# Induced attention and a leaky feed-forward block on one core: a weight quarter loaded later, and a re-planned stage for the first two tiles

## The chip, the cores and the metric

The kernel runs on 1 core of one Trainium2 chip. The metric is the device time of one execution in microseconds (us). PE is the matrix engine (TensorE), ACT the scalar engine (ScalarE), DVE the vector engine (VectorE), POOL the GpSimd engine, and SP the sync engine, whose queue issues nearly all DMAs here.

## The reference

```
B, N, m, C = 4, 12480, 32, 128;  d_ff = 2048;  scale = 1 / sqrt(C)

def mab(q, kv):
    s = scale * (q @ kv^T);  s = s - s.max(-1)
    a = exp(s);  a /= a.sum(-1) + 1e-9
    return a @ kv
h   = mab(inducing, x)             # 32 induced rows of each batch
y   = mab(x, h)                    # attention of all 49920 rows over h
g   = y @ w_in;  g = max(0.01 * g, g)
out = g @ w_out
```

The inputs x and inducing are float32; w_in and w_out come as doubles and are turned into float32 on the chip.

## The kernel before

**What is computed where.** The attention of a row over its batch's 32 induced rows, h, is a softmax weight a of 32 numbers, so `y @ w_in` is `a @ (h @ w_in)`. The kernel makes `hw = h @ w_in` once for each batch, and a product with the first matrix then takes 32 rows of PE's array. Four such products with different hidden blocks f (128 of the 2048 units each) run beside each other on the four row groups of the array; line L1261 (`quarter`) issues these and most of the second products, which are cut into four row groups as well. Operands are kept as a high part and a rest (`ghi`/`glo`, `w_hi`/`w_lo`, `hwhi`/`hwlo`), so a product takes three passes. The slope of 0.01 is a linear term, `w12 = 0.01 * w_in @ w_out`, applied through h (`linear_part`, L1315 in the first stage).

**A tile** is 512 tokens; there are 98 (`NT`), two of them pairs of the batches' remainders. For each tile and f, ACT makes `ghi` from PSUM with a ReLU (L1227). Then either DVE makes `glo` (L1231, the near way), or ACT writes g to SBUF and POOL makes both `ghi` (a cast, L1514) and `glo` (L1516), the far way. `relu` chooses between them by the planner's clocks.

**The order in time.** (1) `first_batch` runs the attention of batch 0 over its rows by a hand-written order: PE transposes row tiles (L748), ACT and DVE copy them to `xT` (L754), PE makes the scores (L410), DVE their maxima (L423, L436, L455), ACT the exponentials, PE the values (L590). Its DMAs are all issued by SP at the start, one after the other: 25 row tiles, and behind those numbered in `LOADS` a quarter of w_in, or the first quarter of w_out. The numbers in `ROUNDS` set where the conversion of the weights from doubles (`from_double`) is put between: for each quarter ACT's `cv_a` (L213), DVE's `cv_b` (L219), `cv_a` (L224), `cv_b` (L231) and `cv_t` (L236), and POOL's sum (L242, into `w_in_sb` or `wraw`). (2) The stage of the first two tiles, `staged`: their first products in rounds of four f, and second products as whole-array matmuls (L1304), with the rest of w_out's conversion, its split (`w_hi` on ACT, L309, `w_lo` on POOL, L313), `w12` (L356) and a softmax of the second tiles (L949 to L999) between. (3) The loop over tiles 2 to 97. Here a planner, run while the program is built, gives every engine its instructions in the order of its own clocks. Work that needs PE's array in another shape (scores L410, values L590, spreads L497) waits until it is gathered into a break of the row-tiled stream; `WAITS` says for each break how long it is put off. (4) A tail for the last tile.

**The planner** does not measure: `spent(engine, ns)` advances a clock by a number written in the code, and these numbers set the order. In `best`, an engine takes what is ready first by them. DVE, ACT and POOL then run their instructions strictly in that order, so a wait of one instruction holds up all behind it.

```
LOADS = [4, 8, 12, 16, 20]
if i in LOADS:
    c = LOADS.index(i)
    raws.append(load_w_in(c) if c < NF // 4 else load_w_out(0))
...
useful = far < max(clock[DVE], start + RELU) + backlog(DVE) + LOW + BEHIND   # in the stage
useful = far <= wanted()                                                     # in the loop
```

Of the kernel before, what the change touches and what calls it, by code (L numbers as in the profile page):

```python
# [19 lines left out]
def induced_attention_then_leaky_ffn(  # L20
# [34 lines left out]
    while N - base >= 4 * TOK:  # L55
# [12 lines left out]
    HEAVY = 2  # L68
    PE, ACT, DVE, POOL, SP = "PE", "ACT", "DVE", "POOL", "SP"

    LOADS = [4, 8, 12, 16, 20]

# [21 lines left out]
    LANDED = 3800.0  # L94
    RELU, LOW, COPIED, ADDED, BLOCKS = 599.0, 691.0, 587.0, 691.0, 702.0
    FAR_HIGH, FAR_LOW, FAR_SUM = 613.0, 1297.0, 1299.0
    SETTLED = 75.0
    EARLY, PREFER, YIELDING, PATIENCE = 250.0, 0.0, 200.0, 6000.0
    IDLE, HURRY, APART, TAIL, WAITING, SOON = 1300.0, 1000.0, 60000.0, 5000.0, 3500.0, 3000.0
# [1 line left out]
    LINEAR = NF - 3  # L101
    SPREAD = 80.0
    WAITS = [
# [3 lines left out]
    ]  # L107
    AHEAD = 100.0
    CLOCKS = {ACT: 1500.0, DVE: 1150.0, POOL: 1800.0}
# [32 lines left out]
    clock = {ACT: 0.0, DVE: 0.0, POOL: 0.0, SP: 0.0}  # L142
# [4 lines left out]
    def spent(engine, ns, *after):  # L147
        if not timing[0]:
            return 0.0
        signal = TO_POOL if engine == POOL else SIGNAL  # L150
        end = max([clock[engine], now[0], *(a + signal for a in after)]) + ns
        clock[engine] = end - OVERLAP[engine]
        return end
# [45 lines left out]
    def from_double(raw, dst):  # L199

        n = dst.shape[1]
        low, high = raw[:, :, 0], raw[:, :, 1]
        a = sb.tile([P, n], I32, tag="aT", name="cv_a", bufs=4)
        b = sb.tile([P, n], I32, tag="aT", name="cv_b", bufs=4)  # L210
        tail = sb.tile([P, n], F32, tag="osb", name="cv_t", bufs=2)
        yield from new(ACT, 0.0)
        nc.scalar.mul(a.bitcast(F32), high.bitcast(F32), 2.0**-112)  # L213
        at = spent(ACT, 700.0)
        if not timing[0]:
            yield
        yield from new(DVE, 0.0)
        spent(DVE, 700.0)
        nc.vector.tensor_scalar(  # L219
            out=b, in0=high, scalar1=-0x80000000, scalar2=None, op0=ALU.bitwise_and  # L220
        )
        yield from old()
        yield from new(DVE, at)
        nc.vector.scalar_tensor_tensor(  # L224
            out=a, in0=a, scalar=3, in1=b, op0=ALU.logical_shift_left, op1=ALU.bitwise_or
        )
        at = spent(DVE, 800.0, at)
        yield from old()
        yield from new(DVE, at)
        spent(DVE, 600.0)  # L230
        nc.vector.tensor_scalar(  # L231
            out=b, in0=a, scalar1=-0x800000, scalar2=None, op0=ALU.bitwise_and
        )
        yield from old()
        yield from new(DVE, 0.0)
        nc.vector.scalar_tensor_tensor(  # L236
            out=tail, in0=low.bitcast(U32), scalar=2.0**-52, in1=b.bitcast(F32),
            op0=ALU.mult, op1=ALU.mult,
        )
        at = spent(DVE, 740.0)  # L240
        yield from new(POOL, at)
        nc.gpsimd.tensor_tensor(out=dst, in0=a.bitcast(F32), in1=tail, op=ALU.add)  # L242
        return spent(POOL, 1280.0, at)

    def words(w):
        return w.bitcast(I32).rearrange("p (n t) -> p n t", t=2)
# [55 lines left out]
    high_w, low_w = [], []  # L302

    def parts_of_w_out():
        for c in range(NF // 4):
            yield from until(lambda: c < len(ready))
            yield from new(ACT, ready[c])
            sl = slice(4 * c, 4 * c + 4)
            nc.scalar.copy(w_hi[:, sl, :], wraws[c])  # L309
            at = spent(ACT, 610.0, ready[c])  # L310
            high_w.append(at)
            yield from new(POOL, at)
            nc.gpsimd.tensor_tensor(  # L313
                out=w_lo[:, sl, :], in0=wraws[c], in1=w_hi[:, sl, :].bitcast(F32), op=ALU.subtract
            )
            low_w.append(spent(POOL, 1290.0, at))
            yield from old()

    winTs, swift = [], [False]
# [256 lines left out]
    middles, scoring, finishing, doing, waiting, blocked = [], [], [1], [0], [0], [False]  # L576
# [607 lines left out]
    high_of, low_of, far_ends = {}, {}, []  # L1184
# [225 lines left out]
    with tc.manual_schedule():  # L1410
        setup()
        late = [chain(setup_w_in(), setup_w_out())]
        turning, splits, twelve = [turn_w_in()], [parts_of_w_out()], [setup_w12()]
# [8 lines left out]
        scaling = [scales()]  # L1422
        one, two, keep = [quick(0)], [quick(1)], lanes["w"]
# [20 lines left out]
        stacking = [stack(s) for s in stacks]  # L1444
        linear = [chain(*turning, *twelve, expand_linear(0))]
        seconds = [second(0, 0, eng=nc.vector)] + [second(0, g) for g in [1, 2, RG, 3, 4, 5]]
# [11 lines left out]
        def follow():  # L1458
# [12 lines left out]
        quads[0] = True  # L1471
        free.extend((released.get(i, 0.0), i) for i in range(8) if i not in held)
        lanes = [
            two, late, splits, linear, scaling, stacking, stores, seconds, values, middles, scores, rests,
        ]
        asks = [(None, 0.0)] * len(lanes)
        asked = [0.0] * len(lanes)
# [15 lines left out]
        def backlog(engine):  # L1493
            return sum(j[1] for j in jobs[engine])

        def relu(t, f, ph, ready, wanted=None):
            _, n = spans(t)
            ghi, glo = live[t, f]
            start = max(clock[ACT], ready + SIGNAL)
            far = max(clock[POOL], start + RELU) + backlog(POOL) + FAR_HIGH + FAR_LOW  # L1500
            left = far_ends[far_open[0] - 2] if far_open[0] < 2 <= len(far_ends) + far_open[0] else 0.0
            if wanted is None:
                useful = far < max(clock[DVE], start + RELU) + backlog(DVE) + LOW + BEHIND
            else:
                useful = far <= wanted()
            if far_open[0] < 2 and left <= start and useful:
                g = sb.tile([P, TOK], F32, tag="g", name="g", bufs=2)
                high(ph, g, n)
                at = spent(ACT, RELU, ready)
                done(ph, at)  # L1510
                far_open[0] += 1

                def on_pool():
                    nc.gpsimd.tensor_copy(ghi[:, :n], g[:, :n])  # L1514
                    high_of[t, f] = spent(POOL, FAR_HIGH, at)
                    nc.gpsimd.tensor_tensor(  # L1516
                        out=glo[:, :n], in0=g[:, :n], in1=ghi[:, :n].bitcast(F32), op=ALU.subtract
                    )
                    low_of[t, f] = spent(POOL, CHAINED + FAR_LOW) + SETTLED
                    far_ends.append(low_of[t, f])  # L1520
                    far_open[0] -= 1

                add(POOL, at, FAR_HIGH + FAR_LOW, on_pool)
                return
            high(ph, ghi, n)
            high_of[t, f] = at = spent(ACT, RELU, ready)

            def rest():
                low(ph, ghi, glo, n)
                low_of[t, f] = spent(DVE, LOW, at)  # L1530
                done(ph, low_of[t, f])

            add(DVE, at, LOW, rest)
# [321 lines left out]
        t = NT - 1  # L1855
# [47 lines left out]
```

## Time and profile before

| What | Value |
|---|---|
| Median of 3 runs | 1426.86 us (1426.69 to 1427.08) |
| Profiled execution | 1428.35 us, span 1426.6 us |
| Busy: PE, DVE, ACT, POOL | 1412.9, 1046.1, 1059.8, 1274.3 us |
| First batch (up to 44 us), PE busy | 37.77 of 44 us |
| Stage of two tiles (44 to 88 us), PE busy | 42.08 of 44 us |
| Loop (88 to 1408 us), PE busy | 1319.82 of 1320 us |
| Tail (1408 to 1426.6 us), PE busy | 13.26 of 18.6 us |

The span runs from the first to the last instruction; the execution's time has 1.75 us more around it. Busy time is what an engine's instructions cover. PE's matmuls are pipelined, so a row group that starves for a short while doesn't show as idle PE; the rate at which the matmuls of L1261 follow each other tells more. A timeline row gives start, duration, engine, line, operation, output and inputs, the count of instructions merged in it, and in brackets the idle time before it with what ended that.

### The profile page before, as it was taken

To read this page: it belongs to the slowest core of one execution; us is meant where nothing else is said; L and a number is where in the kernel's file an instruction comes from. 1 tells how busy PE (TensorE), PEld (TensorE's weight loads), DVE (VectorE), ACT (ScalarE), POOL (GpSimd) and SP (SyncE) were. 2 spreads that over 40 slices of the span, in tenths; PEclk is the share of its full clock that TensorE was granted. 3 is DMA by queue.
4 is the path that set the end of the run, shared out by engine and by line. 5 is a ranking of instruction groups with operands and counts; after the bars stand their busy time and mean duration, and the time that the engine had idled before them with its cause. 6 is when DMAs were issued, how large, how long until landed. Compare 5 with 4: busy or idle time off the path is not lost.

```text
span 1426.6 us, 60356 instructions
## 1 busy us (share of the span) xinstructions
PE 1412.9 (99%) x25179; PEld 1309.7 (92%) x25179; DVE 1046.1 (73%) x1861; ACT 1059.8 (74%) x1957; POOL 1274.3 (89%) x1349
## 2 busy tenths in 40 slices
PE   8999999999999999999999999999999999999998
PEld 6689899988999998998999999899899999999997
DVE  6977877867777787776777878776766766768664
ACT  6667777777777777777777777777787777778775
POOL 1679999989999998889999999999899999989996
PEclk9999999999999999999999999999999999999999
DMA  8164665344544454543643455534233333233331
GB/s 298 19 131 87 106 132 121 75 109 95 104 83 91 80 118 88 108 100 71 128 90 71 96 119 110 109 60 107 54 63 62 60 62 67 47 65 71 57 64 25
DMA packets 400704, 128.50 MB, mean 90 GB/s; under 512 B 373136, under 2 KB 375600, under 8 KB 400432
## 3 DMA queue, kind: packets, MB, share of 16 engines
q1 hardware_dynamic: 399328, 124.50, 42.8%
q8 instruction: 198, 3.24, 1.0%
q14 instruction: 74, 0.61, 0.1%
q10 hardware_dynamic: 1104, 0.15, 0.1%
HBM read 48.94 MB, written 25.56 MB: 52 GB/s over the span
## 4 chain that ended last, share of the span: by engine, by line
PE 97%; DVE 1%; DMA 0%; issue 0%; ACT 0%; SPq 0%; DVEq 0%; ACTq 0%
PE bank L1261 89%; PE bank L410 3%; PE bank L1304 2%; PE bank L590 2%; PE bank L748 1%; DVE glo L1231 0%; DMA xr<-in_x_dram 0%; PE bank L850 0%; PE bank L494 0%; DVE cv_a L224 0%; DVE cv_t L236 0%; PE bank L356 0%; SPq L726 0%; PE bank L497 0%; PE bank L1063 0%
## 5 line engine op out<-in xcount | busy, mean ns | idle before, releaser
L1261 PE MATMUL bank<-ghi,w_hi 32*128 32x512 f32 (+1 forms) x6080 | 1169.6, 375 | 0.0
L1261 PE MATMUL bank<-ghi,w_lo 32*128 32x512 f32 (+1 forms) x6080 | 1169.3, 374 | 0.0
L1261 PE MATMUL bank<-glo,w_hi 32*128 32x512 f32 (+1 forms) x6080 | 1167.6, 374 | 0.0
L1261 PE MATMUL bank<-A,hwhi 32*128 32x512 f32 (+1 forms) x3394 | 990.6, 373 | 0.3 <-ACT A L1106 0.3
L1231 DVE SCALAR_TENSOR_TENSOR glo<-bank,ghi 128x512 fp32r<-128x512 f32 (+1 forms) x997 | 657.3, 681 | 282.5 <-ACT ghi L1227 265.2
L1261 PEld LDWEIGHTS bank<-ghi,w_hi 32*128 32x128 f32 x6080 | 805.6, 184 | 10.8 <-issue 0.6
L1261 PEld LDWEIGHTS bank<-ghi,w_lo 32*128 32x128 f32 x6080 | 803.8, 184 | 9.4 <-issue 1.2
L1261 PEld LDWEIGHTS bank<-glo,w_hi 32*128 32x128 f32 x6080 | 801.7, 184 | 10.4 <-issue 2.2
L1516 POOL TENSOR_TENSOR glo<-g,ghi 128x512 fp32r<-128x512 f32 (+1 forms) x569 | 728.5, 1280 | 45.6
L1227 ACT ACTIVATE ghi<-bank 128x512 fp32r<-128x512 f32 (+1 forms) x997 | 577.1, 597 | 133.9 <-PE bank L1261 113.4
L1261 PE MATMUL bank<-A,hwlo 32*128 32x512 f32 (+1 forms) x1697 | 584.9, 370 | 0.0
L1261 PEld LDWEIGHTS bank<-A,hwhi 32*128 32x128 f32 x3394 | 562.1, 184 | 14.6 <-issue 5.4
L1227 ACT ACTIVATE g<-bank 128x512 f32<-128x512 f32 (+1 forms) x571 | 340.8, 598 | 164.7 <-PE bank L1261 101.6
L1514 POOL CAST ghi<-g 128x512 fp32r<-128x512 f32 (+1 forms) x569 | 349.5, 614 | 38.6 <-ACT g L1227 34.5
L1261 PEld LDWEIGHTS bank<-A,hwlo 32*128 32x128 f32 x1697 | 299.6, 184 | 1.8
L1550 DVE TENSOR_TENSOR part<-bank,part 128x512 f32<-128x512 f32 (+1 forms) x190 | 129.7, 684 | 49.0 <-PE bank L1261 29.6
L1561 POOL TENSOR_TENSOR part<-part 128x512 f32<-128x512 f32 (+1 forms) x95 | 121.6, 1280 | 6.3 <-DVE part L1550 6.2
L1543 ACT COPY part<-bank 128x512 f32<-128x512 f32 (+1 forms) x190 | 110.7, 585 | 10.0 <-PE bank L1261 7.8
L1335 DVE STREAM_TRANSPOSE osb<-part 128x512 f32<-128x512 f32 x93 | 65.2, 701 | 5.7 <-POOL part L1561 4.9
L546 DVE STREAM_TRANSPOSE xT<-xc 128x512 f32<-128x512 f32 x72 | 46.5, 683 | 0.0
L467 ACT ACTIVATE e<-e,nm 128x512 f32<-128x512 f32 (+1 forms) x28 | 18.7, 668 | 27.2 <-DVE least L455 25.0
L966 POOL TENSOR_TENSOR y<-y,mx 128x512 f32<-128x512 f32 (+1 forms) x24 | 24.5, 1022 | 8.2 <-DVE mx L962 7.8
(150 smaller groups left out, 645.9 us busy)
## 6 DMA issues: line engine op xcount, KB each, us to landing
A<-both SPq DMA_DIRECT2D x376, 128.0 KB, 2.4
xr<-in_x_dram SPq DMA_DIRECT2D x96, 256.0 KB, 4.3
out_dram<-osb SPq DMA_DIRECT2D x382, 64.0 KB, 2.2
xc<-in_x_dram SPq DMA_DIRECT2D x288, 64.0 KB, 2.8
raw<-in_moe_w_in_dram SPq DMA_DIRECT2D x4, 512.0 KB, 6.8
raw<-in_moe_w_out_dram SPq DMA_DIRECT2D x4, 512.0 KB, 8.4
A<-both SPq DMA_DIRECT2D x48, 16.0 KB, 1.9
out_dram<-osb SPq DMA_DIRECT2D x48, 8.0 KB, 2.4
```

The costliest lines, as they stand in the source:

```text
L410: nc.tensor.matmul(dst, lhsT, rhs, start=True, stop=True)
L546: nc.vector.transpose(t[:, j, :], blk.rearrange("p n c -> p (n c)"))
L590: nc.tensor.matmul(hp[32 * k : 32 * k + 32, :C], ay[:rows_, 4 * q + k, :], xb[:rows_, k, :], start=(q == 0), stop=(4 * q + 4 >= K), tile_p ...
L1227: nc.scalar.activation(ghi, ph, AF.Relu)
L1231: nc.vector.scalar_tensor_tensor(out=glo, in0=ph, scalar=0.0, in1=ghi, op0=ALU.max, op1=ALU.subtract,)
L1261: nc.tensor.matmul(dst, w[32 * r : 32 * r + 32], woven(x) if turned else x, start=start, stop=stop, tile_position=(32 * r, 0),)
L1335: nc.vector.transpose(osb[:, :n], total[:, :n])
L1514: nc.gpsimd.tensor_copy(ghi[:, :n], g[:, :n])
L1516: nc.gpsimd.tensor_tensor(out=glo[:, :n], in0=g[:, :n], in1=ghi[:, :n].bitcast(F32), op=ALU.subtract)
L1543: nc.scalar.copy(put, got)
L1550: nc.vector.tensor_tensor(out=put, in0=got, in1=put, op=ALU.add)
L1561: nc.gpsimd.tensor_tensor(out=total[:, :n], in0=total[:, :n], in1=part[:, :n], op=ALU.add)
```

## The change

It has four parts. The first quarter of w_out is loaded behind the last row tile of the first batch, no longer behind tile number 20 (`LOADS`). Numbers by which the planner orders the stage are replaced: five durations of the conversion and the split of w_out, a new one, `BESIDE`, that is added to POOL's work for a far split in the stage, and the order of the lanes, which decides between equals. The table `WAITS` is new, with 44 entries in place of 40. The order of all engines from the stage on follows from these. The five replaced durations below are, in this order, those of L219, L224, L236, L242 and L313.

```diff
-    LOADS = [4, 8, 12, 16, 20]
+    LOADS = [4, 8, 12, 16, 24]
...
+    BESIDE = 250.0
...
     WAITS = [
-        6.1, 12.2, 0.1, 0.0, 0.0, 3.4, 6.6, 2.7, 1.0, 7.1, 0.0, 0.8, 6.3, 12.3, 2.9,
+        6.1, 11.1, 0.1, 0.0, 6.7, 3.4, 6.6, 2.7, 1.9, 5.6, 0.0, 0.8, 6.3, 0.0, 3.1, 0.0,
...
-        spent(DVE, 700.0)
+        spent(DVE, 650.0)
-        at = spent(DVE, 800.0, at)
+        at = spent(DVE, 950.0, at)
-        at = spent(DVE, 740.0)
+        at = spent(DVE, 1400.0)
-        return spent(POOL, 1280.0, at)
+        return spent(POOL, 1500.0, at)
...
-            low_w.append(spent(POOL, 1290.0, at))
+            low_w.append(spent(POOL, 1500.0, at))
...
-            two, late, splits, linear, scaling, stacking, stores, seconds, values, middles, scores, rests,
+            two, splits, late, seconds, stacking, linear, scaling, stores, values, middles, scores, rests,
...
-            far = max(clock[POOL], start + RELU) + backlog(POOL) + FAR_HIGH + FAR_LOW
+            far = max(clock[POOL], start + RELU) + backlog(POOL) + FAR_HIGH + FAR_LOW + BESIDE * (wanted is None)
...
-                    high_of[t, f] = spent(POOL, FAR_HIGH, at)
+                    high_of[t, f] = spent(POOL, FAR_HIGH + BESIDE * (wanted is None), at)
```

Below are places where the order of an engine differs. Lines of the changed kernel from L98 on are one higher (L220 is the old L219). A row is a line, an operation, output and inputs, the output's shape, and a count.

SP, the last DMAs of the first batch, before (`xr` are row tiles, `raw` a quarter of a weight in doubles):

```order
L726 DMA xr_147<-in_x_dram 128x512
L277 DMA raw<-in_moe_w_out_dram 128x4x256
L726 DMA xr_151<-in_x_dram 128x512
L726 DMA xr_153<-in_x_dram 128x512
L726 DMA xr_155<-in_x_dram 128x512
L726 DMA xr_157<-in_x_dram 128x512
L277 DMA raw<-in_moe_w_out_dram 128x4x256 x3
```

The same place now:

```order
L727 DMA xr_147<-in_x_dram 128x512
L727 DMA xr_149<-in_x_dram 128x512
L727 DMA xr_151<-in_x_dram 128x512
L727 DMA xr_153<-in_x_dram 128x512
L727 DMA xr_155<-in_x_dram 128x512
L278 DMA raw<-in_moe_w_out_dram 128x4x256 x4
```

The quarter has moved behind four row tiles and stands with the three others of w_out. DVE's order in the first batch is as it was; where that quarter is read first, it is, in the changed kernel (L220 reads `raw`, L755 copies a transposed row tile for the next scores):

```order
L220 TENSOR_SCALAR cv_b<-raw 128x512
L610 SCALAR_TENSOR_TENSOR hacc<-hacc,al,bank_69 128x128
L483 TENSOR_SCALAR zs<-zs,al,zg 128x1
L623 STREAM_TRANSPOSE ay<-e 128x512
L424 TENSOR_SCALAR e,rm<-bank_71 128x512
L437 TENSOR_SCALAR rd,any<-own,rm 128x4
L755 COPY xT<-bank_64 128x512
```

So six instructions of the attention stand behind L220 up to that copy, before as now. POOL in the stage, from the second quarter of w_out on, before:

```order
L242 TENSOR_TENSOR wraw<-cv_a,cv_t 128x512
L1514 CAST ghi<-g 128x512
L1516 TENSOR_TENSOR glo<-g,ghi 128x512
L313 TENSOR_TENSOR w_lo<-wraw,w_hi 128x512
L242 TENSOR_TENSOR wraw<-cv_a,cv_t 128x512
L1514 CAST ghi<-g 128x512
L1516 TENSOR_TENSOR glo<-g,ghi 128x512
```

and now:

```order
L243 TENSOR_TENSOR wraw<-cv_a,cv_t 128x512
L1515 CAST ghi<-g 128x512
L1517 TENSOR_TENSOR glo<-g,ghi 128x512
L314 TENSOR_TENSOR w_lo<-wraw,w_hi 128x512
L1515 CAST ghi<-g 128x512
L1517 TENSOR_TENSOR glo<-g,ghi 128x512
L243 TENSOR_TENSOR wraw<-cv_a,cv_t 128x512
```

The second far split of the stage has moved ahead of the third quarter's sum. DVE at the same time, before:

```order
L1231 SCALAR_TENSOR_TENSOR glo<-bank_66,ghi 128x512
L1231 SCALAR_TENSOR_TENSOR glo<-bank_70,ghi 128x512
L231 TENSOR_SCALAR cv_b<-cv_a 128x512
L236 SCALAR_TENSOR_TENSOR cv_t<-raw,cv_b 128x512
L966 TENSOR_TENSOR y<-y,mx 128x512
L1231 SCALAR_TENSOR_TENSOR glo<-bank_69,ghi 128x512
```

and now:

```order
L1232 SCALAR_TENSOR_TENSOR glo<-bank_70,ghi 128x512
L225 SCALAR_TENSOR_TENSOR cv_a<-cv_a,cv_b 128x512
L967 TENSOR_TENSOR y<-y,mx 128x512
L1157 RECIPROCAL over<-over 128x32
L1232 SCALAR_TENSOR_TENSOR glo<-bank_69,ghi 128x512
L1232 SCALAR_TENSOR_TENSOR glo<-bank_65,ghi 128x512
L367 SCALAR_TENSOR_TENSOR w_80<-bank_68,w_80 128x128
L1232 SCALAR_TENSOR_TENSOR glo<-bank_66,ghi 128x512
L232 TENSOR_SCALAR cv_b<-cv_a 128x512
L237 SCALAR_TENSOR_TENSOR cv_t<-raw,cv_b 128x512
```

The quarter's `cv_b` and `cv_t` stood ahead of the `glo` of bank 69 and now stand behind it and two more. PE at the end of the stage, from the last linear product to the first row-tiled second product, before (the first products of tile 2, twelve rows, are cut to their ends):

```order
L1315 MATMUL bank_67<-A_733,hwhi 128x512
L410 MATMUL bank_64<-xT,hT 32x512 x4
L1261 MATMUL bank_65<-A_1050,hwhi 128x512
...
L1261 MATMUL bank_70<-A_1050,hwhi 128x512
L1304 MATMUL bank_67<-ghi,w_hi 128x512
L1304 MATMUL bank_67<-ghi,w_lo 128x512
L1304 MATMUL bank_67<-glo,w_hi 128x512
L1304 MATMUL bank_67<-ghi,w_hi 128x512
L1304 MATMUL bank_67<-ghi,w_lo 128x512
L1304 MATMUL bank_67<-glo,w_hi 128x512
L1261 MATMUL bank_69<-ghi,w_hi 128x512
```

and now:

```order
L1316 MATMUL bank_67<-A_733,hwhi 128x512
L1262 MATMUL bank_64<-A_1064,hwhi 128x512
...
L1262 MATMUL bank_70<-A_1064,hwhi 128x512
L1305 MATMUL bank_67<-ghi,w_hi 128x512
L1305 MATMUL bank_67<-ghi,w_lo 128x512
L1305 MATMUL bank_67<-glo,w_hi 128x512
L1305 MATMUL bank_67<-ghi,w_hi 128x512
L1305 MATMUL bank_67<-ghi,w_lo 128x512
L411 MATMUL bank_69<-xT,hT 32x512 x4
L1305 MATMUL bank_67<-glo,w_hi 128x512
L1262 MATMUL bank_66<-ghi,w_hi 128x512
```

The four score products L410 have moved from ahead of tile 2's first products to behind them.

## Rows read from the trace of the kernel before

**Rows 1.** The page: busy us of each engine, share of the span, instructions.

```profile
PE 1412.9 (99%) x25179; PEld 1309.7 (92%) x25179; DVE 1046.1 (73%) x1861; ACT 1059.8 (74%) x1957; POOL 1274.3 (89%) x1349
```

**Rows 2.** Windows: length, busy PE, PEld, DVE, ACT, POOL, clock, DMA share, GB/s.

```profile
44.00:88.00 44.00, 42.08 (x310) 29.39 (x312) 38.10 (x65) 25.12 (x51) 32.08 (x34) 1.00 0.33 70
88.00:1408.00 1320.00, 1319.82 (x24389) 1242.80 (x24388) 972.82 (x1688) 1002.61 (x1840) 1225.67 (x1295) 1.00 0.44 87
```

**Rows 3.** Chain that ended last, pieces by time: start us, length us, what.

```profile
84.45 0.99 PE bank L410 x8
...
87.79 16.58 PE bank L1261 x258
...
104.77 30.73 PE bank L1261 x550
...
207.71 38.73 PE bank L1261 x709
```

**Rows 4.** Timeline of SP, the last loads of the first batch.

```profile
20.04 0.39 SPq L277 DMA_DIRECT2D raw<-in_moe_w_out_dram  x1
20.71 2.96 SPq L726 DMA_DIRECT2D xr<-in_x_dram  x4
```

**Rows 5.** From issue to landing, of the load of w_out issued at 20.04.

```profile
DMA to landing us min/median/max: 8.3/8.3/8.3
```

**Rows 6.** The last row tile's issue and landing; the page's median for w_in.

```profile
L726 SPq DMA_DIRECT2D xr<-in_x_dram x1: 328/328/328, 23.4 to 23.4; - x1
DMA to landing us min/median/max: 7.8/7.8/7.8
...
raw<-in_moe_w_in_dram SPq DMA_DIRECT2D x4, 512.0 KB, 6.8
```

**Rows 7.** Timeline of PE in the first batch, the last group's transposes and scores.

```profile
30.19 1.97 PE L748 MATMUL bank<-ident,xr 128*128 128x128 f32 x16
...
32.83 1.06 PE L410 MATMUL bank<-xT,indT 128*32 128x512 f32 x8 [0.36 <-ACT xT L754]
```

**Rows 8.** Timeline of DVE, the same stretch.

```profile
29.68 0.42 DVE L219 TENSOR_SCALAR cv_b<-raw 128x512 int32<-128x512 int32 x1
...
31.95 0.69 DVE L754 COPY xT<-bank 128x512 f32<-128x512 f32 x1
...
33.97 0.69 DVE L423 TENSOR_SCALAR_CACHE_REDUCE e<-bank 128x512 f32<-128x512 f32 x1
```

**Rows 9.** Timeline of ACT, the same stretch.

```profile
30.16 0.67 ACT L213 ACTIVATE cv_a<-raw 128x512 f32<-128x512 f32 x1
```

**Rows 10.** Timeline of PE in the stage, around its two waits.

```profile
57.79 0.38 PE L1304 MATMUL bank<-glo,w_hi 128*128 128x512 f32 x1
59.20 0.48 PE L1304 MATMUL bank<-ghi,w_hi 128*128 128x512 f32 x1 [1.03 <-POOL ghi L1514]
...
62.60 0.38 PE L1304 MATMUL bank<-ghi,w_lo 128*128 128x512 f32 x1
63.85 0.48 PE L1304 MATMUL bank<-glo,w_hi 128*128 128x512 f32 x1 [0.87 <-DVE glo L1231]
```

**Rows 11.** Timeline of POOL ahead of the first of them.

```profile
56.44 1.68 POOL L242 TENSOR_TENSOR wraw<-cv_a,cv_t 128x512 f32<-128x512 f32 x1 [0.64 <-DVE cv_t L236]
58.08 1.07 POOL L1514 CAST ghi<-g 128x512 fp32r<-128x512 f32 x1
```

**Rows 12.** Timeline of ACT: that cast's input, and a cast at the loop's start.

```profile
56.02 0.59 ACT L1227 ACTIVATE g<-bank 128x512 f32<-128x512 f32 x1
...
86.81 0.61 ACT L1019 CAST both<-aT 128x512 fp32r<-128x512 f32 x1
```

**Rows 13.** Timeline of DVE ahead of the second wait.

```profile
60.84 1.75 DVE L236 SCALAR_TENSOR_TENSOR cv_t<-raw,cv_b 128x512 f32<-128x512 uint32 x1
...
63.10 0.69 DVE L1231 SCALAR_TENSOR_TENSOR glo<-bank,ghi 128x512 fp32r<-128x512 f32 x1
```

**Rows 14.** Groups of DVE by line, 10 to 42 us: busy us, mean ns.

```profile
L236 DVE SCALAR_TENSOR_TENSOR cv_t<-raw,cv_b 128x512 f32<-128x512 uint32 x5 | 3.4, 684 | 0.0
```

**Rows 15.** Window in the loop, columns as in rows 2.

```profile
435.00:450.00 15.00, 15.00 (x285) 14.93 (x281) 13.35 (x23) 10.88 (x21) 14.25 (x16) 1.00 0.37 63
```

4 rows, old and new, of the table WAITS are left out of this document.

## The prediction

> **What bounds the kernel now.** I read the engines' busy times first: TensorE (PE) is busy nearly all of the span [rows 1], so only three things can move the time: PE's idle time, work added on PE, and a stretch in which PE's order depends on other engines. The change adds nothing on PE: each order holds 24393 of its instructions, of the same kinds, with 49 breaks between stretches of the row-tiled line L1261. Next the windows by stage [rows 2]. From 88 to 1408 us PE has 0.18 us without work in 1320. In the stage of the first two tiles (44 to 88) it lacks 1.92 of 44 us, and the vector engine DVE is busy 38.10 of them. Before 44 us comes the first batch's attention, a chain of steps on PE, ScalarE (ACT) and DVE. Then the chain of waits, where L1261's pieces give a rate [rows 3]: 38.73 us for 709 matmuls is 54.6 ns each, the settled rate, but the piece at the loop's start takes 16.58 us for 258, 64.3 ns each. At 54.6 it would take 14.09, so 2.5 us are lost there though PE counts as busy. What the change can gain is thus a few us in 1427, and it lies before 105 us.
>
> **First batch: the moved load.** Before, the quarter of w_out is issued at 20.04 and the batch's last four row tiles from 20.71 [rows 4]; it lands 8.3 us later, at 28.4 [rows 5], and the last tile, issued at 23.4, 7.8 us later, at 31.2 [rows 6]. The five now stand as four tiles and then the quarter. They use the same five issue slots and carry the same bytes, so the quarter lands about when the last tile did, at 31.2, and the tiles some 1.4 us earlier. Who needs what? The tiles are read by PE's transposes at 30.19, which follow the products before them without a wait [rows 7]; earlier rows gain nothing there. The quarter is read by DVE's L219 at 29.68 [rows 8] and by ACT's L213 at 30.16 [rows 9], and neither moves in its engine's order. Both would now wait for 31.2: L219 starts 1.55 us later, L213 1.05 later. Behind L219 stand the reading of the next scores' bank, their maxima and L754, a copy that PE's score products L410 need. L754 starts at 31.95 and ends at 32.64; with 1.55 more it ends at 34.2. L410 starts at 32.83 now, released by another of these copies on ACT, and would start at 34.25, 1.4 later. ACT's copies come 1.05 later and so stay hidden behind that. DVE's L423 at 33.97 reads those products, and all that follows to the stage (maxima, exponentials, values, h) hangs on it in one chain. So **+1.4**. Bounds: a load of w_in lands 6.8 us after its issue by the page's median [rows 6]; at that the quarter is there at 30.2, a stall of 0.5 (+0.4 on the path). At its own 8.3 us from the slot at 23.4 it lands at 31.7, +1.9. I take 31.2, which the bytes give.
>
> **The stage.** PE visibly waits twice [rows 10]. Between the starts at 57.79 and 59.20 lie 1.41 us where one product takes 0.22: 1.19 lost, because POOL cast `ghi` at 58.08, behind `wraw` (L242, 56.44 and 1.68 long) [rows 11]. ACT had made its input g at 56.61 [rows 12], and in the new order the cast and its `glo` stand ahead of that L242. A cast from 56.61, even of the 1.07 us that this one took, ends at 57.7, before PE's 58.01, so the wait goes. The second wait is 62.60 to 63.85, 1.03 lost on DVE's `glo`, which starts at 63.10 behind a 1.75 us `cv_t` and the subtraction L966 [rows 13]. In the new order that quarter's `cv_t` stands behind this `glo`, and only the subtraction ahead of it. ACT has its `ghi` one round earlier by the 1.19 already gained, so this goes as well. What is late next: the round of first products with f = 12, whose banks come free by `glo` rows that now stand behind L980 to L988 on DVE. PE has some 4.4 us of work between the round before it and this one (a round of 0.85, eleven products at 0.216, L356's 0.9, changes between them), and DVE's rows in between add up to about the same, so a wait of up to 0.4 us is possible there; it stands against rounds before, at 59.83 and 69.04, that ran some 0.3 longer than others. Work on PE is the same; what moves is which pieces lie between. **-2.2**, with ends of -2.6 (those rounds too) and 0 (both waits come back as others).
>
> **Start of the main loop.** The scores L410 (0.99 us, at 84.45 [rows 3]) ran ahead of tile 2's first products; now they run behind them, between them and the first of their second products. ACT and DVE get 1.0 us more for the first `ghi` and `glo` of tile 2, and ACT no longer has the cast L1019 (0.61 at 86.81 [rows 12]) between them. That can return at most 1.0 + 0.5 of the 2.5 us lost; but the order also starts with fewer first products ahead of the second ones than before, so the rows may starve a little later. From -1.5 to +0.5, I take **-0.6**.
>
> **Waits anew, and the rest of the loop.** The table sets when PE's breaks come. Their number and contents are the same, so their cost is too; the pieces between run at 54.4 to 56 ns before, worth at most some 0.8 us in one piece (30.73 us for 550 is 0.7 over [rows 3]). Sum over the loop: 0, from -1 to +1. The tail from 1408 us has the same order on PE: 0.
>
> **Sum.** +1.4 - 2.2 - 0.6 + 0 = -1.4 us in the profiled execution's 1428.35 (span 1426.6, 1.75 around it). The runs' median is 1426.86, 1.5 below that one; the change is set against the median: **1425.5**. A difference below 0.2%, 2.85 us, is about what a measurement of this kernel can't tell from none, so 1424.0 and 1429.7 are the marks.
>
> **Rivals.** (B) The quarter's place costs nothing: it lands before it is asked for, or DVE finds slack. Then -2.2 - 0.6 = -2.8, 1424.1. For it: SP issues it only 3.3 us later, and the eight outstanding transfers could finish out of order. Against: the landings at 28.4 and 31.2 follow the issue order, and DVE shows no idle time from L219 to L754. The Trainium skill (DMA: Bandwidth & Descriptors, Queues, rings and completion order) says that completion is not first-in-first-out for an issuing engine, though each DMA engine takes descriptors in ring order; by its first half B holds, by its second the quarter stays behind the tiles, and the two landings here go with the second.
>
> (C) The stage's waits come back in other places, so only the late quarter is left: +1.4, and -0.2 at the loop's start, 1428.1, slower. The mechanism is POOL and DVE holding each other up: `cv_t` takes 684 ns in the first batch [rows 14] but 1.75 us at 60.84 beside POOL's work [rows 13]. The new order puts POOL's casts and `glo` earlier, beside other DVE work. It decides if a `glo` that PE asks for is held up by more than about 1 us. Against: DVE's `glo` reads one operand from PSUM and keeps 0.68 us beside POOL; it only inherits the delay of the rows ahead, and I have allowed 1.75 for each `cv_t`. The Trainium skill (SBUF — State Buffer, Who interferes with whom) has a rule that speaks for C: a DVE instruction with two SBUF inputs and a GpSimd one that reads SBUF lock each other out for a whole instruction. The trace agrees (0.68 against 1.75); by it no order removes the total, only its place.
>
> (D) The loop itself gets worse. In the new order POOL makes 511 splits in place of 561 and DVE 1025 in place of 975; 26 of the 50 fall in nine tiles, about 920 to 1040 us. At 0.68 us each that is 17.8 us more for DVE in 120. If PE lost there what it lost in the stage (2.2 in 44 us, with DVE at 87%), it would lose 6 us; with half of it and A's -1.4, 1428.5 to 1431.5, about 1430, slower. It decides when DVE passes some 90%. Against: from 435 to 450 us DVE is busy 13.35 of 15 and PE never idles [rows 15]; the stretch in question would reach about that.
>
> **Chances.** Forecast (A) 0.60, with a range of its own of 1423.8 to 1427.2; B 0.17; C 0.14; D 0.09. Faster by over 0.2%: 0.08 from A's lower edge and 0.09 from B (about half of it), 0.17. Slower: 0.06 from D, 0.03 from C's upper edge, 0.09. Within: 0.74. The range that should hold 8 in 10 leaves out B's lower half and D: 1423.2 to 1428.7.
>
> **What would show it.** Right: DVE's L220 (the old L219) for the first quarter of w_out starts near 31.2 after a wait on a transfer, the fourth group's score products near 34.2, the stage's first L1262 near 45.4; PE has no wait over 0.5 us in the stage, and the loop's first L1262 piece begins near 86.8 and runs under 64 ns a matmul. Wrong: no wait at L220 (B); new waits on `glo` or `ghi` of about 1 us between 55 and 75 (C); pieces between 920 and 1040 us over 56 ns (D). A loop that runs several us faster or slower elsewhere would show that the table of waits does something I read as nothing.

## The result: slower, and the loss is in the loop

The changed kernel takes 1434.37 us (1433.63 to 1436.17), the kernel before beside it 1427.12 (1426.69 to 1427.59): a ratio of 1.0053 (95% interval 1.0040 to 1.0066), 7.25 us more. Forecast were 1425.5, with 1428.7 as the upper end. The profiled execution has a span of 1432.7 us, 6.1 more than before's.

The page of the profile after, which answers to [rows 1] (busy us, share of the span, instructions of each engine), shows PE as full as before, DVE with more splits and POOL with fewer:

```profile
PE 1418.2 (99%) x25179; PEld 1299.0 (91%) x25179; DVE 1071.8 (75%) x1911; ACT 1061.9 (74%) x1957; POOL 1185.7 (83%) x1249
```

The same two windows as [rows 2], after. The stage has gained PE time; in the long window PE still has work at nearly every moment, yet does 105 instructions fewer than before in the same 1320 us:

```profile
44.00:88.00 44.00, 43.43 (x323) 30.55 (x323) 38.34 (x66) 26.68 (x54) 32.63 (x36) 1.00 0.26 55
88.00:1408.00 1320.00, 1319.91 (x24284) 1227.87 (x24285) 995.04 (x1734) 998.80 (x1828) 1131.49 (x1188) 1.00 0.44 87
```

Pieces of the chain after (start us, length us, what), against [rows 3]. Line numbers are one higher than before, so L1262 is the row-tiled line:

```profile
87.39 27.99 PE bank L1262 x457
...
115.74 23.45 PE bank L1262 x414
...
145.69 9.29 PE bank L1262 x156
...
213.86 36.77 PE bank L1262 x663
```

That is 61.2, 56.6, 59.6 and 55.5 ns for each quarter, where before's piece at 207.71 ran at 54.6. Split by the starts of PE's instructions, the profiled pair gives: the stage begins at 45.22 us (43.94 before, +1.28); it is 42.10 long (43.78, -1.67); the loop is 1327.35 long (1320.80, +6.55); behind it nothing differs. The loop is made of breaks, 61.49 us (61.77 before), and of pieces of the row-tiled line, 1265.87 us (1259.03, **+6.84** for the same 23202 quarters).

### What a slow piece looks like

The timeline of PE, first before in a settled stretch and then after at a change of tiles (start us, length us, line, out<-in):

```profile
119.74 0.37 PE L1261 MATMUL bank<-A,hwhi 32*128 32x512 f32 x1
119.74 0.37 PE L1261 MATMUL bank<-glo,w_hi 32*128 32x512 f32 x1
119.91 0.37 PE L1261 MATMUL bank<-ghi,w_hi 32*128 32x512 f32 x1
119.95 0.37 PE L1261 MATMUL bank<-ghi,w_lo 32*128 32x512 f32 x1
119.96 0.37 PE L1261 MATMUL bank<-glo,w_hi 32*128 32x512 f32 x1
119.96 0.37 PE L1261 MATMUL bank<-A,hwhi 32*128 32x512 f32 x1
```

```profile
103.57 0.37 PE L1262 MATMUL bank<-glo,w_hi 32*128 32x512 f32 x1
103.68 0.37 PE L1262 MATMUL bank<-A,hwlo 32*128 32x512 f32 x1
103.79 0.37 PE L1262 MATMUL bank<-ghi,w_hi 32*128 32x512 f32 x1
103.90 0.37 PE L1262 MATMUL bank<-A,hwhi 32*128 32x512 f32 x1
104.00 0.37 PE L1262 MATMUL bank<-ghi,w_lo 32*128 32x512 f32 x1
...
104.33 0.37 PE L1262 MATMUL bank<-ghi,w_hi 32*128 32x512 f32 x1
```

Before, four quarters start in every 0.22 us, one for each row group. After, from 103.57 on, they start 0.11 apart: two groups work and two stand still, and because each quarter is recorded as 0.37 us long, PE still counts as busy. ACT and DVE in that stretch, after, show what the idle groups lacked, a free bank for the next tile's sum:

```profile
103.08 1.07 ACT L1544 COPY part<-bank 128x512 f32<-128x512 f32 x2
104.03 0.63 ACT L1228 ACTIVATE ghi<-bank 128x512 fp32r<-128x512 f32 x1
```

```profile
103.70 1.29 DVE L1551 TENSOR_TENSOR part<-bank,part 128x512 f32<-128x512 f32 x2 [0.89 <-ACT part L1544]
```

The sums of the old tile leave their banks only with L1544 and L1551, and in the kernel's order the two idle groups' next quarters write the two banks that L1544's copies empty. The first of these copies ends near 103.66, yet the quarter that needs its bank starts at 104.33: in PE's order the two groups' next quarters stand 25 and 22 places behind their last ones, and the queue is worked off in that order. The Trainium skill (TensorEngine Tiling (Array Packing), Performance Considerations, and Gotcha 1) says that row tiling speeds up TensorE but not the emptying of PSUM, and raises the pressure on it; this stretch agrees, with 1.07 us for ACT's two copies and 1.29 for DVE's two sums.

Such places can be counted in PE's order. A group's turn is every fourth quarter. A group **passes over** two or more turns if its next quarter stands nine or more places behind its last one. The kernel before has 15 such places, the changed kernel 45. So a sign of this loss, though not its size, could be seen in the order, ahead of any run.

How much of the loss lies at these places can be worked out by putting the recorded starts of the quarters beside PE's order, which says the group of each. A group that is never idle starts a 512-column quarter every 0.216 us. What it takes beyond that between two of its quarters in one piece, divided by the four groups, is PE time lost. Summed over the loop this estimate gives 11.1 us before and 18.0 after, so idle groups account for the whole of the 6.84. The passed-over turns hold 2.1 us of it before and 6.2 after, which is 4.0 of the 6.9; the other 2.9 lies in shorter gaps, which the count doesn't see.

### The profile page after: what moved, and what is told of

It reads as the page before. It is cut to its first block, busy times and chain, and to the rows that moved or that the text cites. A ratio compares the mean times of both kernels' runs of the same rounds, so it can differ in the third digit from the quotient of the medians.

```text
span 1432.7 us, 60191 instructions
## 1 busy us (share of the span) xinstructions
PE 1418.2 (99%) x25179; PEld 1299.0 (91%) x25179; DVE 1071.8 (75%) x1911; ACT 1061.9 (74%) x1957; POOL 1185.7 (83%) x1249
## 4 chain that ended last, share of the span: by engine, by line
PE 95%; DMA 2%; DVE 2%; issue 0%; SPq 0%; ACT 0%; DVEq 0%; ACTq 0%
PE bank L1262 88%; PE bank L411 3%; PE bank L1305 2%; PE bank L591 1%; DMA xr<-in_x_dram 1%; DVE glo L1232 1%; DMA raw<-in_moe_w_in_dram 1%; DMA raw<-in_moe_w_out_dram 0%; PE bank L851 0%; SPq L727 0%; DVE cv_a L225 0%; DVE cv_b L220 0%; PE bank L357 0%; PE bank L498 0%; PE bank L1064 0%
## 5 line engine op out<-in xcount | busy, mean ns | idle before, releaser
L1262 PE MATMUL bank<-glo,w_hi 32*128 32x512 f32 (+1 forms) x6080 | 1167.9, 374 | 0.0
L1262 PE MATMUL bank<-ghi,w_hi 32*128 32x512 f32 (+1 forms) x6080 | 1166.7, 375 | 0.0
L1262 PE MATMUL bank<-ghi,w_lo 32*128 32x512 f32 (+1 forms) x6080 | 1164.6, 374 | 0.0
L1262 PE MATMUL bank<-A,hwhi 32*128 32x512 f32 (+1 forms) x3394 | 991.0, 374 | 0.4 <-ACT A L1107 0.3
L1232 DVE SCALAR_TENSOR_TENSOR glo<-bank,ghi 128x512 fp32r<-128x512 f32 (+1 forms) x1047 | 686.5, 681 | 236.4 <-ACT ghi L1228 219.7
L1262 PEld LDWEIGHTS bank<-ghi,w_lo 32*128 32x128 f32 x6080 | 812.5, 184 | 13.7 <-issue 2.4
L1262 PEld LDWEIGHTS bank<-ghi,w_hi 32*128 32x128 f32 x6080 | 809.4, 184 | 16.2 <-issue 1.6
L1262 PEld LDWEIGHTS bank<-glo,w_hi 32*128 32x128 f32 x6080 | 812.2, 184 | 12.5 <-issue 1.2
L1228 ACT ACTIVATE ghi<-bank 128x512 fp32r<-128x512 f32 (+1 forms) x1047 | 607.9, 598 | 156.4 <-PE bank L1262 132.9
L1517 POOL TENSOR_TENSOR glo<-g,ghi 128x512 fp32r<-128x512 f32 (+1 forms) x519 | 664.3, 1280 | 41.6
L1262 PE MATMUL bank<-A,hwlo 32*128 32x512 f32 (+1 forms) x1697 | 585.7, 370 | 0.0
L1262 PEld LDWEIGHTS bank<-A,hwhi 32*128 32x128 f32 x3394 | 563.3, 184 | 16.3 <-issue 2.7
L1228 ACT ACTIVATE g<-bank 128x512 f32<-128x512 f32 (+1 forms) x521 | 311.2, 598 | 145.7 <-PE bank L1262 88.2
L1515 POOL CAST ghi<-g 128x512 fp32r<-128x512 f32 (+1 forms) x519 | 316.8, 610 | 116.9 <-ACT g L1228 90.4
L1262 PEld LDWEIGHTS bank<-A,hwlo 32*128 32x128 f32 x1697 | 300.3, 184 | 2.7
L1551 DVE TENSOR_TENSOR part<-bank,part 128x512 f32<-128x512 f32 (+1 forms) x190 | 129.9, 685 | 75.3 <-PE bank L1262 37.6
L1544 ACT COPY part<-bank 128x512 f32<-128x512 f32 (+1 forms) x190 | 110.8, 584 | 8.3 <-PE bank L1262 6.5
L1027 POOL TENSOR_TENSOR both<-aT,both 128x512 fp32r<-128x512 f32 x24 | 31.2, 1298 | 0.2
```

The costliest lines, as they stand in the source:

```text
L1027: (eng or nc.gpsimd).tensor_tensor(out=alo[sl], in0=aT.pop((b, g))[: 32 * J, :], in1=ahi[sl].bitcast(F32), op=ALU.subtract,)
L1228: nc.scalar.activation(ghi, ph, AF.Relu)
L1232: nc.vector.scalar_tensor_tensor(out=glo, in0=ph, scalar=0.0, in1=ghi, op0=ALU.max, op1=ALU.subtract,)
L1262: nc.tensor.matmul(dst, w[32 * r : 32 * r + 32], woven(x) if turned else x, start=start, stop=stop, tile_position=(32 * r, 0),)
L1517: nc.gpsimd.tensor_tensor(out=glo[:, :n], in0=g[:, :n], in1=ghi[:, :n].bitcast(F32), op=ALU.subtract)
L1544: nc.scalar.copy(put, got)
```

## Experiments

Each column of the table is read from one profiled execution (stage: from the first to the loop's first L1261 or L1262; loop: to the end of its last long piece), but for the time, which is the median of the timed runs, and the last two, which are counted in the orders of PE and POOL (the stage's splits among them).

| run | time us | ratio (95%) | stage begins | stage | loop | its pieces | its breaks | passed over | POOL splits |
|---|---|---|---|---|---|---|---|---|---|
| before | 1427.1 to 1427.3 | | 43.94 | 43.78 | 1320.80 | 1259.03 | 61.77 | 15 | 571 |
| load_alone | 1430.83 | 1.0024 (1.0014 to 1.0033) | 45.68 | 43.76 | 1321.45 | 1259.74 | 61.71 | 15 | 571 |
| changed | 1434.37 | 1.0053 (1.0040 to 1.0066) | 45.22 | 42.10 | 1327.35 | 1265.87 | 61.49 | 45 | 521 |
| load_back | 1433.49 | 1.0043 (1.0030 to 1.0056) | 43.48 | 42.77 | 1327.66 | 1266.17 | 61.49 | 45 | 521 |
| new_table_old_stage | 1436.97 | 1.0068 (1.0056 to 1.0081) | 42.69 | 43.76 | 1330.70 | 1268.52 | 62.18 | 65 | 562 |
| old_table_new_stage | 1466.82 | 1.0278 (1.0264 to 1.0292) | 44.46 | 42.78 | 1358.52 | 1295.13 | 63.39 | 77 | 515 |
| lanes_alone | 1439.28 | 1.0084 (1.0071 to 1.0098) | 42.46 | 42.99 | 1333.47 | 1271.02 | 62.45 | 54 | 575 |
| refit_load_back | 1428.65 | 1.0010 (1.0001 to 1.0019) | 41.57 | 42.77 | 1322.90 | 1260.08 | 62.82 | 15 | 537 |
| refit_load_late | 1430.66 | 1.0025 (1.0015 to 1.0035) | 44.75 | 42.77 | 1322.71 | 1259.89 | 62.82 | 15 | 537 |
| one_entry | 1429.60 | 1.0018 (1.0009 to 1.0027) | 43.38 | 43.70 | 1323.47 | 1261.57 | 61.91 | 20 | 571 |
| refit_second | 1427.20 | 1.0000 (0.9991 to 1.0009) | 42.16 | 42.06 | 1321.84 | 1260.54 | 61.30 | 27 | 564 |

**load_alone.** The kernel before, with

```
-    LOADS = [4, 8, 12, 16, 20]
+    LOADS = [4, 8, 12, 16, 24]
```

> The kernel before with the quarter of w_out issued four row tiles later, and nothing else; the order on every engine but SP is that of before. If the load has its own price, as the first batch of the changed kernel shows (its stage begins 1.28 us later), and a shift of the whole loop is harmless: 1427.1 + 1.3 = 1428.4 us, ratio 1.0009 (1.0003 to 1.0015). If the loop is upset by where it begins against the transfers and the other engines' state: several us more, up to 1434.

Measured 1430.83, +3.5 by the medians; in the profile the stage begins 1.74 later and the loop is 0.65 longer. The loop isn't upset, and the run is slower by more than the 1.3 expected. In this profiled execution some 1.2 of the 1.74 isn't the load: PE's granted clock was 0.57 from 34 to 38 us, and the stage begins 15.5 us after the quarter has landed, against 14.3 in the other three traces with the late load.

**load_back.** The changed kernel, with

```
-    LOADS = [4, 8, 12, 16, 24]
+    LOADS = [4, 8, 12, 16, 20]
```

> The changed kernel with the quarter of w_out back at its old place in the queue; the order of the loop stays that of the changed kernel. If the loop's loss lies in the order of the loop: 1434.4 - 1.3 = 1433.1 us, ratio 1.0042. If the late load is the root of the loss: about 1426.5, since then only the stage's gain of 1.7 us is left, with some at the loop's start.

Measured 1433.49: 0.9 back, and the loop keeps its 1327.66. The late load is not the root of the loss.

**new_table_old_stage.** The kernel before with the new table alone:

```
-        6.1, 12.2, 0.1, 0.0, 0.0, 3.4, 6.6, 2.7, 1.0, 7.1, 0.0, 0.8, 6.3, 12.3, 2.9,
...
+        6.1, 11.1, 0.1, 0.0, 6.7, 3.4, 6.6, 2.7, 1.9, 5.6, 0.0, 0.8, 6.3, 0.0, 3.1, 0.0,
...
```

> The kernel before with the new table of waits alone. Theory T (the table itself costs: the breaks fall where the row groups then starve): 1427.1 + 5 to 6.5 = 1432 to 1433.6 us, the loss spread as in the changed kernel (half of it before 570 us). Theory S (the loop's loss comes from what the new stage hands over: fewer first products ahead and another share of the splits, so that any table fares badly): within 1 us of before, 1426 to 1428.

Measured 1436.97, and the loop 9.9 longer. S, in which only the new stage harms, falls. The size is above T's, and the loss lies elsewhere than in the changed kernel. Timed by the count of quarters done, about 7 of the 9.9 us are lost behind 800 us here, while the changed kernel has lost 4.4 of its 6.5 before 570.

**old_table_new_stage.** The changed kernel with the old table, the same lines with - and + exchanged.

> The changed kernel with the old table of waits. The order now has 54 breaks of the row-tiled stream in place of 48, at other places. Theory T: the loss of the loop goes but for the six more breaks (each adds the change between two kinds of work, some 0.3 us: up to 2 us), so 1428 to 1430 us. Theory S: the loss stays, 1434 us or more; if a table that was made for another stage does harm of its own, above 1435.

Measured 1466.82, far above both. T, by which the old table was the good one, falls too. Some 17 us of it have a cause of their own. The waits of PE between 1332 and 1446 us (engine, line, releaser, total us, times, longest):

```profile
PE bank L1262 <- DMA A<-both: 11.0, 1, 11.0
```

PE stands for 11.0 us, up to 1344.78, for the transfer that fills A (why it comes so late there was not followed up). Its granted clock falls within this wait and stays down for 8.5 us behind it (windows, columns as in [rows 2]):

```profile
1333.00:1336.00 3.00, 0.78 (x5) 0.34 (x2) 1.78 (x4) 1.22 (x2) 1.85 (x2) 1.00 0.00 0
1336.00:1339.00 3.00, 0.00 (x0) 0.00 (x0) 1.74 (x5) 0.00 (x0) 1.47 (x2) 0.54 0.14 22
1344.78:1353.30 8.52, 8.22 (x41) 5.35 (x45) 3.93 (x7) 3.26 (x6) 0.00 (x0) 0.50 0.71 155
```

The 41 instructions of the last window would take 2.2 us at 54.6 ns each, so 6.3 us more are lost there. At half the rate they would take 4.5, so the clock is 2.2 of the 6.3; what holds the rest up was not followed.

From these two runs a third theory came, K: a table is worth what PE's order under it is worth, and it fits only the timeline of the stage for which it was found. The passed-over turns should show it.

**refit_load_back.** The changed kernel with the load back and a table found by counting passed-over turns in the order:

```
-    LOADS = [4, 8, 12, 16, 24]
+    LOADS = [4, 8, 12, 16, 20]
...
-        6.1, 11.1, 0.1, 0.0, 6.7, 3.4, 6.6, 2.7, 1.9, 5.6, 0.0, 0.8, 6.3, 0.0, 3.1, 0.0,
...
+        11.5, 11.5, 7.0, 5.5, 0.0, 4.0, 10.0, 2.7, 1.9, 5.6, 1.2, 4.0, 6.3, 4.0, 0.0,
...
```

> The changed kernel with its load back at the old place and with a third table of waits, chosen so that in PE's order a row group seldom passes over its turn: 15 times a group's next quarter stands nine or more places behind its last one (four is its turn), as in the kernel before (15); the changed kernel has 45 such places, the new table on the old stage 65. POOL makes 537 splits. Theory K (the loop's loss is these skipped turns, about 0.2 us each beyond before's 15): the loop is as before, the stage's gain of 1.7 us stays, 1425.4 us (1424 to 1427). Theory D (POOL's smaller share of the splits is the loss, 0.13 us for each of the 50 moved to DVE): 34 fewer than before, so +4.4 - 1.7 = 1430. Theory S (the new stage hands over a state in which any table fares badly): 1431 or more.

Measured 1428.65, above K's 1427 and below the others. The stage is the new one, and the pieces are back at 1260.08 us from 1266.17: the loss in the loop goes with the table alone. What is missing against K, in the profiles: the breaks are 1.3 us longer than load_back's, since this table makes breaks begin that then wait (PE waits 1.3 us in five places of the loop, where load_back has no such wait); the pieces are still 1.0 longer than before's; and the stage gives 1.0, not 1.7.

**refit_load_late.** The same with the load at 24.

> The same with the quarter of w_out behind all row tiles of the first batch, as the change has it; PE's order is the same. Theory K: 1.0 to 1.3 us above the run with the load back, so 1426.7 us (1425 to 1428): the change with this table would be no slower than before. If the late load also upsets the loop, as the +3.5 of the load alone would have it: 1428 to 1429.

Measured 1430.66, above both; against the run with the load back it is 2.0, where 1.0 to 1.3 were expected. With a table that fits, the change as it stands loses 3.4 us in place of 7.2, and most of that is the load.

**lanes_alone.** The kernel before with the new order of the planner's lanes:

```
-            two, late, splits, linear, scaling, stacking, stores, seconds, values, middles, scores, rests,
+            two, splits, late, seconds, stacking, linear, scaling, stores, values, middles, scores, rests,
```

> The kernel before with only the new order of the lanes (the list of side jobs that the planner picks from); load, durations and table as before. 48 breaks, as before; POOL makes 575 splits, more than before's 571; a row group passes over two or more turns 54 times in place of 15. Theory K: 39 more at 0.2 us, 1427.1 + 8 = 1435 us (1433 to 1437). Theory D: more splits on POOL, so no loss: 1425.5 to 1427.5. Theory T (the table is what costs): the table is that of before, 1427.

Measured 1439.28. D falls: POOL does more than before (575 splits; the page of this run has it at 1280.5 us, above [rows 1]), and the loop is 12.7 us longer.

```profile
PE 1420.4 (99%) x25179; PEld 1314.3 (91%) x25179; DVE 1046.3 (73%) x1857; ACT 1067.5 (74%) x1957; POOL 1280.5 (89%) x1357
```

The table is that of before, so it isn't the table by itself either. K is right in sign and 4 us short in size. Some 3.2 of these lie at the loop's start in this profiled execution and are no passed-over turns: between 86 and 100 us PE stands idle for 1.5 us, and a clock of 0.88 is worth 1.7 (window, columns as in [rows 2]):

```profile
86.00:100.00 14.00, 12.47 (x172) 11.02 (x168) 10.06 (x19) 10.40 (x19) 12.46 (x13) 0.88 0.71 164
```

**one_entry.** The kernel before with one wait of 40 changed:

```
-        2.2, 1.7, 0.0, 11.1, 0.0, 8.5, 2.2, 4.9, 4.0, 1.4,
+        2.2, 2.2, 0.0, 11.1, 0.0, 8.5, 2.2, 4.9, 4.0, 1.4,
```

> The kernel before with one of the 40 entries of its table changed from 1.7 to 2.2 us, a break near the end of the second third. PE's order is that of before up to about 870 us; behind it the planner's decisions fall otherwise: 20 places where a row group passes over two or more turns in place of 15, and 49 breaks in place of 48. Theory K: 5 more at 0.2 us and one more break at 0.4 to 1 us, so 1427.3 + 1.5 to 2.5 = 1429 us (1428.5 to 1430), all of it behind 870 us. Theory T (a break costs by its place, and one break that moves by 0.5 us is nothing): 1427.3, within 0.5.

Measured 1429.60, inside K's range and outside T's. The place was off: the chain of this run still has before's counts at 975.78 (292) and parts from it in the next piece, which has 176 quarters where before has 164:

```profile
975.78 15.99 PE bank L1261 x292
...
992.82 9.72 PE bank L1261 x176
...
1006.62 15.56 PE bank L1261 x263
```

The last piece runs at 59.2 ns, though nothing near it but one break's start has changed, and eight matmuls that followed that break at once now make a break of their own at 1022.19.

**refit_second.** As refit_load_back, with a fourth table, placed so that PE finds operands ready at its breaks too:

```
-        6.1, 11.1, 0.1, 0.0, 6.7, 3.4, 6.6, 2.7, 1.9, 5.6, 0.0, 0.8, 6.3, 0.0, 3.1, 0.0,
...
+        1.5, 0.0, 7.0, 5.5, 11.0, 4.0, 11.0, 9.0, 1.9, 5.0, 9.0, 4.0, 9.0, 4.0, 0.0,
...
```

> The changed kernel with its load back and with a fourth table of waits. A row group passes over two or more turns 27 times, between refit_load_back's 15 and the changed kernel's 45; POOL makes 564 splits. Theory K by the count: the loop is 12 x 0.2 = 2.4 us longer than refit_load_back's 1322.6, 1325; the whole 1428.65 + 2.4 = 1431 us (1429.5 to 1432). If the count is only a sign of stalls and not their measure (this table's breaks were placed to find PE's operands ready, so its breaks themselves stall less): as refit_load_back or below, 1426.5 to 1428.5. Theory D: 27 more splits on POOL than refit_load_back, 0.13 us each, 1425.

Measured 1427.20. K's size fails here: 12 more passed-over turns than refit_load_back cost 0.46 us in the pieces, not 2.4, and the breaks give 1.5 back. The count tells tables with 45 or more such places from those with 27 or fewer; within a group it is no measure. By the estimate above, the passed-over turns do cost 1.1 us more here (3.5 against 2.4), but the shorter gaps cost 0.5 less, which the count can't see. Pieces of this run's chain, at the loop's start still slow (63.0 ns), then 55.1 and 55.6:

```profile
84.30 23.25 PE bank L1262 x369
...
123.11 22.04 PE bank L1262 x400
...
147.27 18.41 PE bank L1262 x331
```

No version here beats the kernel before; this one equals it, and is 6.3 us below load_back, from which it differs by the table alone.

## Why the prediction was wrong

**The step that failed** is "Waits anew, and the rest of the loop", taken at 0 from -1 to +1. Its first half held: the breaks' number and contents are the same and cost 61.49 us against 61.77. The second half did not: it read the table as something that only places breaks, and priced the pieces between them by the rate that before's pieces happen to have. The table also sets what the planner puts into the pieces, which group's quarter comes when above all: 45 passed-over turns in place of 15. The pieces lost 6.84 us, and with another table 6.1 of it came back in the same stage (refit_load_back). I noted that the order "starts with fewer first products ahead" and gave it 0.5 us at most; whether that had a part in the loss no run tells apart.

**First batch, +1.4.** The mechanism was as forecast. SP's issues, then DVE and PE after, against [rows 4], [rows 8] and [rows 7]:

```profile
19.22 5.21 SPq L727 DMA_DIRECT2D xr<-in_x_dram  x6
24.78 2.59 SPq L278 DMA_DIRECT2D raw<-in_moe_w_out_dram  x4
```

```profile
31.04 0.43 DVE L220 TENSOR_SCALAR cv_b<-raw 128x512 int32<-128x512 int32 x1 [1.67 <-DMA raw<-in_moe_w_out_dram]
```

```profile
33.43 0.38 PE L495 MATMUL bank<-rd,e 128*128 128x4 f32 x2 [1.66 <-DVE rd L437]
34.12 1.07 PE L411 MATMUL bank<-xT,indT 128*32 128x512 f32 x8 [0.31 <-DVE least L456]
...
45.22 0.49 PE L1262 MATMUL bank<-A,hwhi 32*128 32x512 f32 x4 [0.31 <-ACT A L1107]
```

L220 starts at 31.04 behind a transfer (forecast 31.2), the scores at 34.12 (34.2), the stage at 45.22 (45.4). But the size came from one execution. The seven traces with the early load begin the stage at 41.57 to 43.94 us, mean 42.8, and before's is the last of them; the four with the late load begin it at 44.46 to 45.68, mean 45.0, and 44.8 without load_alone, whose clock was down for part of it. So the load costs some 2.0 us; the medians of the three pairs (3.5, 0.9, 2.0) give 2.1. Rival B, that it is hidden, is out. The scatter is that of the landings. With the early load the stage begins 12.5 us after the last row tile has landed (29.1 to 31.0) in six traces, and 12.75 after it (31.2) in before's; with the late load it begins 14.3 us after the quarter has landed (30.2 to 30.9) in three of four. So "earlier rows gain nothing there" was read from the one execution in which the last tile wasn't quite what set the pace.

**Stage, -2.2.** PE's wait on POOL's `ghi` is gone in all six traces of the new stage. The wait on DVE's `glo` is 0.2 in two of them, and 1.17 in the other four, as here in refit_load_back:

```profile
60.71 0.48 PE L1305 MATMUL bank<-glo,w_hi 128*128 128x512 f32 x1 [1.17 <-DVE glo L1232]
```

So the stage gives 1.0 in four and 1.7 in two, where 2.2 was forecast: the first half of the step held, and rival C holds for the second wait in most executions.

**Start of the loop, -0.6.** It begins at 87.39 (forecast 86.8). The first two pieces take 51.44 us for 871 quarters; at 54.6 ns they would take 47.56, so 3.9 are lost there. Before, its first two pieces [rows 3] took 47.31 for 808, 3.2 lost. That is +0.7 in place of -0.6, part of the +6.84.

**Rival D** had the sign and a price near the truth, and the wrong place. From 920 to 1040 us the two longest pieces are not slow (chain, after: 54.3 and 54.7 ns), though DVE took its splits there, and lanes_alone lost more while POOL made four splits more than before:

```profile
923.71 41.08 PE bank L1262 x756
...
985.08 21.86 PE bank L1262 x400
```

The windows of this stretch, before and then after (columns as in [rows 2]): DVE is at 80%, and PE does as many instructions as before, 2241 against 2238:

```profile
920.00:1040.00 120.00, 120.00 (x2238) 111.66 (x2238) 82.81 (x147) 91.46 (x170) 111.86 (x119) 1.00 0.37 80
920.00:1040.00 120.00, 119.95 (x2241) 108.51 (x2237) 95.88 (x171) 91.04 (x166) 67.54 (x69) 1.00 0.37 80
```

DVE isn't blameless there: from 1026.5 to 1032.7 the chain runs through its splits and sums. But by the estimate above idle groups cost 1.2 us in the whole stretch against 0.8 before, not 6.

The sum, by the profiled pair: +1.28 - 1.67 + 6.55 = +6.16, and the spans differ by 6.1. The medians differ by 7.25, since before's profiled execution had a slow first batch. What stays open is why a given table makes few or many groups stand idle. The runs show that it does, and that each of these two tables, put under the other's stage, lost more than at home.

## What to carry to other kernels

A table of numbers that was fitted to a planner belongs to everything ahead of it: after any edit upstream, price the whole order anew, and don't read "same instructions, same breaks" as the same time. Where several row groups are fed from one queue, a busy PE hides idle groups (here 1319.91 us busy of 1320 in a loop that had lost 6.55), so look at ns per piece. Before forecasting, count in the new order how often a group passes over its turns; the count warns, and doesn't give the price. A step that hangs on a load's landing wants several executions: here the stage's start scattered by 2.4 us with the same program ahead of it.

## What the hardware showed that was not expected

Whether PE's second wait in the stage comes back goes with which of two engines runs long when they start within 0.03 us of each other. The order of DVE and POOL there is the same in these two traces. In refit_load_back POOL's L243 starts at 56.09 and DVE's L220 at 56.10; L220 then takes 1.54 us:

```profile
56.09 1.27 POOL L243 TENSOR_TENSOR wraw<-cv_a,cv_t 128x512 f32<-128x512 f32 x1
```

```profile
56.10 1.54 DVE L220 TENSOR_SCALAR cv_b<-raw 128x512 int32<-128x512 int32 x1
```

In refit_second POOL starts at 56.67 and L220 at 56.70; now L220 takes 0.47 and POOL 1.65, and PE's wait is 0.19 in place of 1.17:

```profile
56.67 1.65 POOL L243 TENSOR_TENSOR wraw<-cv_a,cv_t 128x512 f32<-128x512 f32 x1
```

```profile
56.70 0.47 DVE L220 TENSOR_SCALAR cv_b<-raw 128x512 int32<-128x512 int32 x1
```

The Trainium skill (SBUF — State Buffer, Who interferes with whom) says that a port which DVE and GpSimd share is an exclusive lock for a whole instruction, that a tensor_scalar can take it, and that the order of issue decides who blocks. The four durations agree; the recorded starts don't show who was first, since POOL's is the earlier one in both. The other four traces of the new stage go one way or the other: in three L220 takes 1.53 or 1.54 us and POOL 1.27, with a wait of 1.2, and in the changed kernel's L220 takes 0.48 and POOL 1.64, with a wait of 0.2.

While PE stood for 11.0 us in old_table_new_stage, its granted clock fell to 0.50, the lower of its two levels (1.2 of 2.4 GHz), and was still there for the first 8.5 us of work behind the wait, which cost some 2.2 us by the rates above.
